# Gated mix of linear attention and feed-forward: the first loads cut into halves of rows over two queues

## The chip, the cores and the metric

The kernel runs on one core of a Trainium2 chip. The metric is device time in microseconds (us) of one execution, the median of several runs; lower is better. Beside the times there is one profiled execution, with every instruction of every engine and the traffic of the DMA queues.

## The reference

For one sequence of 2048 tokens of width 640 the kernel mixes two branches with a gate per token:

```python
qkv = x @ wqkv                                   # 32 heads of 20
phi(t) = concat(softmax(t @ w_phi), softmax(-t @ w_phi))
kv, z = phi(k).T @ v, sum over tokens of phi(k)  # linear attention
a = (phi(q) @ kv / (phi(q) @ z + 1e-6)) @ wo
b = silu(x @ w1) @ w2                            # width 1728
g = sigmoid(sum(x * gate_w))
out = g * a + (1 - g) * b
```

All inputs and the output are float32.

## The kernel before

Every float32 operand of a large product is split into a rounded part ("hi") and the remainder ("lo"), and each product is made of three passes, hi by hi, hi by lo and lo by hi (`PASSES`, line 57). `split` (line 113) does this: ScalarE (ACT) copies the source into the rounded tile, then VectorE (DVE) or GpSimd (POOL) subtracts it from the source. TensorE (PE) multiplies, SyncE (SP) issues nearly all loads.

The kernel has three long stages: keys and values of 16 token tiles with their sums, then the feed-forward branch, then queries, attention and output. The change touches the very beginning of the first stage, lines 342 to 382, where the work is written out in order and `inorder` (line 122) holds PE, ACT, DVE and POOL to that order.

What stands there:

- Eight matmuls on a tile of ones (`warm`, line 284) run first; they need no input.
- `xT` is read in chunks of 128 of the 640 input features (c = 0 to 4), 256 tokens at a time. `x_loads` (line 162) is a generator: each `next(x0)` loads one chunk (`xra`, 128 KB) and splits it into `xa`, lo on POOL.
- `wv` holds the value weights and the gate column, 642 columns. Chunk 0 of it is the tile `wvr0`, called wv0 here (lines 343, 344, 347): the first 360 columns are loaded by the ACT queue, the other 282 by SP.
- The key weights are not read ready-made: `wkc` (320 KB a chunk) and `wkr` (the last heads, 48 rows) are multiplied on PE with a block-diagonal matrix of `w_phi` in `k_weights` (line 296, tile `pwk`), and the result is split into columns 0 to 639 of `wh` and `wl`. The block-diagonal matrix is expanded by one DVE instruction (line 355) from `bdc`.
- The order on PE is: values of chunk 0 for tokens 0 to 255 (`share(0, ...)`, twelve matmuls into `kvp` and `kvq`, in the three passes), key weights of chunk 0 (`pwk`, twelve matmul records), values of chunk 1, key weights of chunk 1, and so on. `v_weights` (line 328) loads the value weights of chunks 1 to 4 (`wvr1` to `wvr4`, 321 KB each) on SP.

Loads signal their landing on eight DMA semaphores in turn (DMAHW0 to DMAHW7), so a load's issuing instruction waits until the load eight places earlier in the program has landed.

Of the kernel before, what the change touches and what calls it, by code (L numbers as in the profile page):

```python
# [8 lines left out]
F32 = mybir.dt.float32  # L9
# [7 lines left out]
P = 128  # L17
S = 2048
D = 640
# [31 lines left out]
EB = 2  # L51
KXB = 1
WC = 2 * D + 2
CUTS = (0, 500, 1000, WC)
# [6 lines left out]
def mix_kernel(ctx: ExitStack, tc: tile.TileContext, xT, wqT, wkc, wkr, wv, bd, bdc, cst, wo, w1, w1r, w2, out):  # L61
    nc = tc.nc
# [6 lines left out]
    def opened(name, **kw):  # L69
        open_pools[name] = tc.tile_pool(name=name, bufs=1, **kw)  # L70
        return open_pools[name].__enter__()
# [7 lines left out]
    ta = opened("ta")  # L79
# [14 lines left out]
    def raw(name):  # L94
        return wp.tile([P, D + 2], F32, tag="raw", name=name, bufs=4)

    def slot(name, pool=None, tag="x", bufs=7):
        return (pool or wp).tile([P, 2, 512], F32R, tag=tag, name=name, bufs=bufs)
# [14 lines left out]
    def split(hi, lo, src, lo_eng="dve"):  # L113
        nc.scalar.copy(hi, src)  # L114
        eng = nc.vector if lo_eng == "dve" else nc.gpsimd
        eng.tensor_tensor(lo, src, hi.bitcast(F32), op=ALU.subtract)  # L116
# [4 lines left out]
    @contextmanager  # L121
    def inorder(*engines):

        traced = nc.cur_bb.bb.instructions
        n = len(traced)
        yield
        prev = {}
        for i in traced[n:]:
            if i.engine in engines:
                if i.engine in prev:  # L130
                    tc.add_manual_dep(
                        i,
                        prev[i.engine],
                        mybir.DependencyInfo(mybir.DependencyClass.NoSync, mybir.DependencyReason.DATA),
                        reason="inorder",
                    )
                prev[i.engine] = i.name
# [7 lines left out]
    warms = cp.tile([P, 1], F32, name="warms")  # L145
# [3 lines left out]
    st0 = [t[:, k * D : (k + 1) * D] for t in stf for k in range(3)][:NC]  # L149
# [3 lines left out]
    onesf = ta.tile([P, P], F32, name="onesf")  # L153
# [4 lines left out]
    g_d = dp.tile([NT, P], F32, name="g_d")  # L158

    X = {}  # L160

    def x_loads(phase, u, tiles=None):

        tiles = [] if tiles is None else tiles
        for c in range(0, NC, 1 if phase == "f" else 2):
            r = raw(f"xr{phase}_{u}_{c}")[:, :512]
            t = slot(f"x{phase}_{u}_{c}")
            if phase == "f":
                nc.sync.dma_start(r, xT[c * P : (c + 1) * P, u * 512 : (u + 1) * 512])
                split(t[:, 0, :], t[:, 1, :], r)  # L170
                tiles.append(t)
            else:
                n = min(2, NC - c)
                tiles += [t[:, :, k * 256 : (k + 1) * 256] for k in range(n)]
                step = n if u else 1
                for k in range(0, n, step):
                    cols = slice(k * 256, (k + step) * 256)
                    nc.sync.dma_start(
                        r[:, cols].rearrange("p (c s) -> p c s", s=256),
                        xT[(c + k) * P : (c + k + step) * P, u * 256 : (u + 1) * 256].rearrange("(c p) s -> p c s", p=P),  # L180
                    )
                    split(t[:, 0, cols], t[:, 1, cols], r[:, cols], "pool")
                    if k + step < n:
                        yield
            yield
        X["f" if phase == "f" else "t", u] = tiles

    def load_x(phase, u):
        for _ in x_loads(phase, u):
            pass  # L190

    def x_of(t):
        return [x[:, :, t % 2 * P : (t % 2 + 1) * P] for x in X["t", t // 2]]

# [14 lines left out]
    def xb_split(p):  # L209
# [4 lines left out]
        if c == 0:  # L214
            X["t", u] = []
        X["t", u].extend(t[:, :, k * 256 : (k + 1) * 256] for k in range(r.shape[1] // 256))

# [78 lines left out]
    def k_weights(c, half):  # L296

        g0, g1 = ((0, 4), (4, GR))[half]
        bank = ps.tile([P, 512], F32, tag=f"pwk{half}", name=f"pwk{c}_{half}", bufs=2 - half)
        for gi in range(g0, g1):  # L300
            n = min(GW, D - gi * GW)
            r = st0[c][:n, gi * P : (gi + 1) * P] if gi < NG else strest[:n, c * P : (c + 1) * P]
            lo = (gi - g0) * GW
            nc.tensor.matmul(bank[:, lo : lo + n], r, bdt[:n, gi, :n], start=True, stop=True)  # L304
        return bank

    def k_split_w(c, half, bank):
        lo, hi = ((0, 4 * GW), (4 * GW, D))[half]
        split(wh[:, c, lo:hi], wl[:, c, lo:hi], bank[:, : hi - lo])

    def kv_share(c, todo):

        for hx, hw in PASSES:
            for t, lo, hi, opens in todo:
                nc.tensor.matmul(  # L315
                    kv_cols(t, lo, hi),
                    x_of(t)[c][:, hx, :],
                    WKV[hw][:, c, lo:hi],
                    start=(opens and hx == 0 and hw == 0),
                    stop=(c == NC - 1 and hx == 1),  # L320
                    skip_group_check=True,
                )

    X["t", 0] = []
    x0 = x_loads("a", 0, X["t", 0])
    kvp1 = [None] + [ps.tile([P, 512], F32, name=f"kvq{k}") for k in (1, 2)]

    def v_weights(c):
        r = ta.tile([P, 2 * D], F32, tag="e", name="wvr1", bufs=EB)[:, : D + 2] if c == 1 else flat(f"wvr{c}") if c == 2 else raw(f"wvr{c}")
        nc.sync.dma_start(r, wv[c * P : (c + 1) * P, :])  # L330
        split(WKV[0][:, c, D:], WKV[1][:, c, D:], r)

    def values(t):
        return [(t, D, CUTS[2]), (t, CUTS[2], WC)]

    def keys(t):
        return [(t, 0, CUTS[1]), (t, CUTS[1], D)]

    def share(c, cols, opens=()):
        kv_share(c, [(*p, p in opens) for p in cols])  # L340

    with inorder(PE, ACT, DVE, POOL):
        wv0 = ta.tile([P, 2 * D], F32, tag="e", name="wvr0", bufs=EB)[:, : D + 2]
        nc.scalar.dma_start(wv0[:, : CUTS[2] - D], wv[:P, : CUTS[2] - D])
        nc.scalar.dma_start(st0[0], wkc[0])
        next(x0)
        nc.sync.dma_start(wv0[:, CUTS[2] - D :], wv[:P, CUTS[2] - D :])
        nc.sync.dma_start(bdct, bdc)
        nc.sync.dma_start(strest[: wkr.shape[0], :], wkr)
        for lo, hi in ((D, CUTS[2]), (CUTS[2], WC)):  # L350
            split(WKV[0][:, 0, lo:hi], WKV[1][:, 0, lo:hi], wv0[:, lo - D : hi - D])
        cols = [p for pair in zip(values(0), values(1)) for p in pair]
        share(0, cols, cols)
        blocks = bdt[:, :, :GW].rearrange("p g (j f) -> p g j f", f=DH)
        nc.vector.tensor_tensor(
            blocks,
            bdct[:GW, : GR * DH].rearrange("p (g f) -> p g f", f=DH)[:, :, None, :].to_broadcast([GW, GR, GR, DH]),
            bdct[:GW, GR * DH :][:, None, :, None].to_broadcast([GW, GR, GR, DH]),
            op=ALU.mult,
        )  # L360
        for c in range(NC):
            if c + 1 < NC:
                next(x0)
                v_weights(c + 1)
                nc.sync.dma_start(st0[c + 1], wkc[c + 1])
            for half in range(2):
                k_split_w(c, half, k_weights(c, half))
            if c == 0:
                share(1, values(0) + values(1))
            elif c < 3:  # L370
                share(c - 1, keys(0), keys(0)[:1] if c == 1 else ())
            else:
                share(c - 1, [(0, lo, hi) for lo, hi in zip(CUTS, CUTS[1:])])
        share(NC - 1, [(0, lo, hi) for lo, hi in zip(CUTS, CUTS[1:])])
        kvp1[0] = ps.tile([P, 512], F32, tag="pwk0", name="kvq0", bufs=2)
        for k, (lo, hi) in enumerate(zip(CUTS, CUTS[1:])):
            for c in range(NC):
                if c > 1 or k == 0:
                    kv_share(c, [(1, lo, hi, c == 0)])
                elif k == 1:  # L380
                    kv_share(c, [(1, lo, D, False)])
        load_x("a", 1)
# [180 lines left out]
    phs, eks = {}, {}  # L563
    X["f", 0] = []
    xf0 = x_loads("f", 0, X["f", 0])
    with inorder(ACT, DVE, POOL):
        for t in range(NT - 1):
# [123 lines left out]
    r = raw("w1rr")  # L691
# [4 lines left out]
    r = raw("w2rr")  # L696
# [637 lines left out]
```

## Time and profile before

| what | us |
|---|---|
| median of 3 runs (lowest, highest) | 764.87 (764.68, 765.44) |
| the profiled execution's own time | 765.65 |
| its span, first to last instruction | 763.9 |
| PE busy | 757.3 |
| first matmul on real data starts | 5.59 |
| second half of wv0 is cast | 6.15 |
| first key-weight matmul starts | 8.17 |

The span begins with the first instruction; times in the rows are microseconds from there. A line of the timeline gives start, duration, engine, line, operation, output and inputs with their shapes, and in brackets how long the engine had idled before and what released it. ACTq and SPq are the instructions with which those engines issue DMAs; they are not counted as busy.

### The profile page before, as it was taken

The page shows a single profiled execution, that of the slowest core. Times are in us where ns is not written, and L with a number is a line of the kernel's source. Part 1 is how long each engine was busy: PE and PEld are TensorE (multiplying, and loading weights), DVE is VectorE, ACT ScalarE, POOL GpSimd, SP SyncE. Part 2 cuts the span into 40 slices and gives each one's busy share as a digit, 9 for nine tenths or more (in the row PEclk, how much of TensorE's full clock was granted, in tenths as well). Part 3 has the DMA queues.
Part 4 walks back from the last instruction along what each step waited for, and adds up shares of the span by engine and source line. Part 5 has one row for each costly group of instructions (what it writes and reads, how often), then busy time and mean ns, then how long its engine had stood idle before and what let it go on. Part 6 is the DMA issues. An engine that isn't in the chain of part 4 may idle for free.

```text
span 763.9 us, 10660 instructions
## 1 busy us (share of the span) xinstructions
PE 757.3 (99%) x4259; PEld 666.6 (87%) x4259; DVE 370.3 (48%) x662; ACT 267.5 (35%) x484; POOL 263.0 (34%) x163
## 2 busy tenths in 40 slices
PE   8999999999999999999999999999999999999998
PEld 7888888888888888888888888888899999999998
DVE  5676666676641221112211122123587888787761
ACT  5444444336542211122211222133454443334341
POOL 2488777758000000000000000001166766855641
PEclk9999999999999999999999999999999999999999
DMA  7111111112650220002200025022004222111222
GB/s 254 52 53 53 52 52 53 60 46 85 206 174 1 70 82 1 1 0 72 84 0 1 1 68 160 17 65 86 15 1 158 91 75 71 53 52 43 70 70 91
DMA packets 35454, 50.36 MB, mean 66 GB/s; under 512 B 3539, under 2 KB 23267, under 8 KB 35405
## 3 DMA queue, kind: packets, MB, share of 16 engines
q1 hardware_dynamic: 35117, 49.18, 20.5%
q8 instruction: 33, 0.54, 0.3%
q10 hardware_dynamic: 288, 0.51, 0.3%
q14 instruction: 16, 0.13, 0.1%
HBM read 38.56 MB, written 11.11 MB: 65 GB/s over the span
## 4 chain that ended last, share of the span: by engine, by line
PE 92%; POOL 2%; DVE 2%; DMA 2%; issue 1%; ACT 1%; SPq 0%; POOLq 0%; DVEq 0%
PE acc L684 22%; PE ph L503 22%; PE kvp L456 16%; PE pa L1069 9%; PE pq L414 8%; PE pn L1026 3%; PE kv L426 2%; PE pT L951 2%; PE kvp L519 2%; PE kvp L315 1%; PE kvq L315 1%; PE pwk L304 1%; POOL eq L813 1%; POOL ez L777 1%; DMA wvr<-wv 1%
## 5 line engine op out<-in xcount | busy, mean ns | idle before, releaser
L116 POOL TENSOR_TENSOR xb<-xrb,xb 128x512 fp32r<-128x512 f32 (+1 forms) x18 | 19.9, 1130 | 342.1 <-ACT xb L114 338.4
L116 DVE TENSOR_TENSOR u<-ph,u 128x512 fp32r<-128x512 f32 x48 | 33.2, 691 | 178.0 <-ACT u L114 177.9
L684 PE MATMUL acc<-u,w 128*128 128x512 f32 x480 | 114.8, 392 | 0.1
L684 PEld LDWEIGHTS acc<-u,w 128*128 128x128 f32 x480 | 89.5, 188 | 19.3 <-ACT u L114 0.5
L503 PE MATMUL ph<-xf,w 128*128 128x512 f32 x420 | 99.8, 390 | 0.0
L505 ACT ACTIVATE ph<-ph 128x512 f32<-128x512 f32 x48 | 27.9, 582 | 189.2 <-PE ph L503 189.2
L503 PEld LDWEIGHTS ph<-xf,w 128*128 128x128 f32 x420 | 78.7, 188 | 16.7
L456 PE MATMUL kvp<-wh,xa 128*128 128x500 f32 (+1 forms) x420 | 93.0, 357 | 0.0
L456 PEld LDWEIGHTS kvp<-wh,xa 128*128 128x128 f32 x420 | 71.6, 188 | 9.8
L1069 PE MATMUL pa<-oT,wo 120*128 120x256 f32 x600 | 76.8, 282 | 0.0
L1069 PEld LDWEIGHTS pa<-oT,wo 120*128 120x128 f32 x600 | 73.7, 188 | 0.0
L684 PE MATMUL acc<-u,f 128*128 128x512 f32 x300 | 73.3, 394 | 0.0
L503 PE MATMUL ph<-xf,f 128*128 128x512 f32 x300 | 72.7, 394 | 0.0
L503 PEld LDWEIGHTS ph<-xf,f 128*128 128x128 f32 x300 | 56.4, 188 | 13.1
L684 PEld LDWEIGHTS acc<-u,f 128*128 128x128 f32 x300 | 56.2, 188 | 13.0
L777 POOL TENSOR_TENSOR ez<-eq,zbc 128x1280 f32<-128x1280 f32 x16 | 48.0, 3000 | 38.3 <-ACT eq L763 38.0
L116 POOL TENSOR_TENSOR ph<-ek,ph 128x1280 fp32r<-128x1280 f32 x16 | 47.5, 2966 | 27.9 <-ACT ph L114 27.9
L414 PE MATMUL pq<-wq,xb 128*128 128x320 f32 x360 | 55.4, 311 | 0.0
L414 PEld LDWEIGHTS pq<-wq,xb 128*128 128x128 f32 x360 | 53.0, 188 | 0.0
L456 PE MATMUL kvp<-wl,xa 128*128 128x500 f32 (+1 forms) x210 | 47.4, 356 | 0.0
L813 POOL TENSOR_TENSOR eq<-eq,sm 128x1280 f32<-128x1280 f32 x16 | 37.9, 2367 | 21.1 <-DVE sm L807 17.6
L484 POOL TENSOR_TENSOR ek<-ek,st 128x1280 f32<-128x1280 f32 x16 | 37.9, 2369 | 9.2 <-issue 6.1
(159 smaller groups left out, 1105.2 us busy)
## 6 DMA issues: line engine op xcount, KB each, us to landing
wr<-w SPq DMA_DIRECT2D x26, 320.0 KB, 3.1
xrf<-xT SPq DMA_DIRECT2D x20, 256.0 KB, 3.6
fb_d<-o SPq DMA_DIRECT2D x20, 256.0 KB, 2.3
y<-fb_d SPq DMA_DIRECT2D x16, 256.0 KB, 3.2
out<-y SPq DMA_DIRECT2D x16, 256.0 KB, 2.3
xra<-xT SPq DMA_DIRECT2D x14, 256.0 KB, 2.6
xrb<-xT SPq DMA_DIRECT2D x12, 256.0 KB, 2.7
xra<-xT SPq DMA_DIRECT2D x12, 128.0 KB, 2.9
```

What stands on the lines that cost most here:

```text
L116: eng.tensor_tensor(lo, src, hi.bitcast(F32), op=ALU.subtract)
L315: nc.tensor.matmul(kv_cols(t, lo, hi), x_of(t)[c][:, hx, :], WKV[hw][:, c, lo:hi], start=(opens and hx == 0 and hw == 0), stop=(c == NC - ...
L414: nc.tensor.matmul(dst, xt[c][:, hx, :], w[:, c, hw, lo : lo + n], start=first, stop=(hx == 1 and c == NC - 1))
L456: nc.tensor.matmul(kv_cols(t, lo, hi), xt[c][:, hx, :], WKV[hw][:, c, lo:hi], start=(n == 0), stop=(n == 3 * NC - 1), skip_group_check=True,)
L484: nc.gpsimd.tensor_tensor(groups(e), groups(e), spread(st[:, 1, :]), op=ALU.mult)
L503: nc.tensor.matmul(ph, lhs, rhs, start=(n == 0), stop=(n == len(todo) - 1))
L505: nc.scalar.activation(hs, ph, AF.Silu)
L684: nc.tensor.matmul(acc[m], lhs, rhs, start=(f == order[0] and n == 0), stop=(f == order[-1] and n == len(todo) - 1))
L777: nc.gpsimd.tensor_tensor(ez, Q[t]["e"], zbc, op=ALU.mult)
L813: nc.gpsimd.tensor_tensor(groups(q["e"]), groups(q["e"]), spread(q["sm"][:, 2 * H : 4 * H]), op=ALU.mult)
L1026: nc.tensor.matmul(pns[u, gp][:GW, a, :], kvw_of(hk, 2 * i + jj)[:w], f[:w, hp, jj * 256 : (jj + 1) * 256], start=(n == 0), stop=(n == 3 * ...
L1069: nc.tensor.matmul(pa[:, a, :], WO[:GW, c, hw, ds] if c < NG else WOR[:, ds], o[:, ho, c, :], start=(k == 0), stop=(k == len(todo) - 1),)
```

## The change

The tile of wv0 is made earlier. A helper `both` issues a load as two, rows 0 to 63 on SP and rows 64 to 127 on ACT. The first chunk of `xT` and the whole of wv0 are loaded that way, wv0 behind the chunk on both queues. `wkc` of chunk 0 moves from the ACT queue to SP, behind `bdc` and ahead of `wkr`. ACT gets a one-column copy into `warms` ahead of its first cast. The split of wv0 keeps its two column parts.

```diff
     X = {}
+    wv0 = ta.tile([P, 2 * D], F32, tag="e", name="wvr0", bufs=EB)[:, : D + 2]
+
+    def both(dst, src):
+
+        for eng, rows in ((nc.sync, slice(0, P // 2)), (nc.scalar, slice(P // 2, P))):
+            eng.dma_start(dst[rows], src[rows])
 
     def x_loads(phase, u, tiles=None):
...
                 for k in range(0, n, step):
                     cols = slice(k * 256, (k + step) * 256)
-                    nc.sync.dma_start(
-                        r[:, cols].rearrange("p (c s) -> p c s", s=256),
-                        xT[(c + k) * P : (c + k + step) * P, u * 256 : (u + 1) * 256].rearrange("(c p) s -> p c s", p=P),
-                    )
+                    if u == 0 and c + k == 0:
+                        both(r[:, cols], xT[:P, :256])
+                    else:
+                        nc.sync.dma_start(
+                            r[:, cols].rearrange("p (c s) -> p c s", s=256),
+                            xT[(c + k) * P : (c + k + step) * P, u * 256 : (u + 1) * 256].rearrange(
+                                "(c p) s -> p c s", p=P
+                            ),
+                        )
+                    if u == 0 and c + k == 0:
+                        both(wv0, wv[:P, :])
+                        nc.scalar.copy(warms, onesf[:, :1])
                     split(t[:, 0, cols], t[:, 1, cols], r[:, cols], "pool")
...
     with inorder(PE, ACT, DVE, POOL):
-        wv0 = ta.tile([P, 2 * D], F32, tag="e", name="wvr0", bufs=EB)[:, : D + 2]
-        nc.scalar.dma_start(wv0[:, : CUTS[2] - D], wv[:P, : CUTS[2] - D])
-        nc.scalar.dma_start(st0[0], wkc[0])
         next(x0)
-        nc.sync.dma_start(wv0[:, CUTS[2] - D :], wv[:P, CUTS[2] - D :])
         nc.sync.dma_start(bdct, bdc)
+        nc.sync.dma_start(st0[0], wkc[0])
         nc.sync.dma_start(strest[: wkr.shape[0], :], wkr)
```

SP's queue at the beginning, before. `xra` is the input chunk, `wvr` value weights, `stage` the space for key weights, `bdc` and `wkr`:

```order
L178 DMA xra_0_125<-xT 128x256
L347 DMA wvr_122<-wv 128x282
L348 DMA stage_93<-bdc 128x126
L349 DMA stage_92<-wkr 48x640
L178 DMA xra_0_125<-xT 128x256
L330 DMA wvr_153<-wv 128x642
L365 DMA stage_92<-wkc 128x640 [waits DMAHW0_49]
L178 DMA xra_2_182<-xT 128x256 [waits DMAHW1_49]
```

The same place with the change:

```order
L166 DMA xra_0_123<-xT 64x256
L166 DMA wvr_100<-wv 64x642
L358 DMA stage_93<-bdc 128x126
L359 DMA stage_92<-wkc 128x640
L360 DMA stage_92<-wkr 48x640
L187 DMA xra_0_123<-xT 128x256
L344 DMA wvr_155<-wv 128x642 [waits DMAHW0_49]
L376 DMA stage_92<-wkc 128x640 [waits DMAHW1_49]
L187 DMA xra_2_184<-xT 128x256 [waits DMAHW2_49]
```

`wkc` of chunk 0 stands ahead of the second input chunk, there is one load more in all, and so the load of `wvr1` (L344) now waits for DMAHW0, the first half of the first input chunk; before, it waited for nothing.

ACT at the beginning, its two loads and its first casts, before (`wh<-wvr_122` is wv0, `wh<-wvr_153` is `wvr1`):

```order
L344 DMA wvr_122<-wv 128x360
L345 DMA stage_92<-wkc 128x640
L114 ACT_TABLE_LOAD
L114 CAST xa_0_126<-xra_0_125 128x256 [waits DMAHW1_49]
L114 CAST wh<-wvr_122 128x360 [waits DMAHW0_49]
L114 CAST wh<-wvr_122 128x282 [waits DMAHW2_49]
L114 CAST xa_0_126<-xra_0_125 128x256 [waits DMAHW6_49]
L114 CAST wh<-wvr_153 128x642 [waits DMAHW7_49]
```

With the change:

```order
L166 DMA xra_0_123<-xT 64x256
L166 DMA wvr_100<-wv 64x642
L195 ACT_TABLE_LOAD
L195 COPY warms<-onesf 128x1 [waits DVE_49]
L114 CAST xa_0_124<-xra_0_123 128x256 [waits DMAHW1_49,DMAHW0_49]
L114 CAST wh<-wvr_100 128x360 [waits DMAHW3_49,DMAHW2_49]
L114 CAST wh<-wvr_100 128x282
L114 CAST xa_0_124<-xra_0_123 128x256 [waits DMAHW7_49]
L114 CAST wh<-wvr_155 128x642 [waits DMAHW0_49]
```

The table load stands where it stood, third on the engine. The first cast of wv0 waits for both halves of its rows, all columns; the second waits for nothing more. On PE, DVE and POOL the order of the computing instructions is that of before, from first to last. On SP, near the end of the program, one load of a partial sum from `fb_d` stands ahead of one output store that it used to follow.

## Rows read from the trace of the kernel before

**Rows 1.** The page, part 1: busy time, share of the span, instructions.

```profile
PE 757.3 (99%) x4259; PEld 666.6 (87%) x4259; DVE 370.3 (48%) x662; ACT 267.5 (35%) x484; POOL 263.0 (34%) x163
```

**Rows 2.** Chain of waits from 0 to 60: start us, us, what.

```profile
1.19 4.93 DMA wvr<-wv
...
6.63 0.39 PE kvp L315
```

**Rows 3.** Waits of PE, whole run: total us, times, longest us.

```profile
PE kvp L315 <- ACT wh L114: 1.2, 2, 0.8
...
PE pn L1026 <- DVE fT L969: 0.4, 1, 0.4
```

**Rows 4.** Timeline from 0 to 11: start us, us, what, [idle before, releaser].

```profile
1.05 3.78 PE L284 MATMUL warm<-ones 128*128 128x512 f32 x8 [1.05 <-DVE ones L154]
...
1.64 1.28 ACT L114 ACT_TABLE_LOAD   x1 [1.64 <-PEq L1325]
...
3.10 0.43 SPq L330 DMA_DIRECT2D wvr<-wv  x1
4.57 0.33 SPq L365 DMA_DIRECT2D stage<-wkc  x1
4.75 0.40 ACT L114 CAST xa<-xra 128x256 fp32r<-128x256 f32 x1 [1.82 <-DMA xra<-xT]
...
5.06 0.49 ACT L114 CAST wh<-wvr 128x360 fp32r<-128x360 f32 x1
5.23 0.73 POOL L116 TENSOR_TENSOR xa<-xra,xa 128x256 fp32r<-128x256 f32 x1 [3.93 <-ACT xa L114]
5.58 0.78 DVE L116 TENSOR_TENSOR wl<-wvr,wh 128x360 fp32r<-128x360 f32 x1 [3.67 <-ACT wh L114]
...
5.59 0.43 PE L315 MATMUL kvp<-wh,xa 128*128 128x360 f32 x1 [0.76 <-ACT wh L114]
...
6.15 0.43 ACT L114 CAST wh<-wvr 128x282 fp32r<-128x282 f32 x1 [0.61 <-DMA wvr<-wv]
...
6.61 0.45 DVE L116 TENSOR_TENSOR wl<-wvr,wh 128x282 fp32r<-128x282 f32 x1 [0.26 <-ACT wh L114]
...
6.98 0.90 DVE L355 TENSOR_TENSOR stage<-stage 120x720 f32<-120x720 f32 x1
...
7.91 0.73 ACT L114 CAST wh<-wvr 128x642 fp32r<-128x642 f32 x1 [0.41 <-DMA wvr<-wv]
...
8.17 1.61 PE L304 MATMUL pwk<-stage,stage 120*128 120x120 f32 x12
...
8.67 0.83 DVE L116 TENSOR_TENSOR wl<-wvr,wh 128x642 fp32r<-128x642 f32 x1 [0.79 <-ACT wh L114]
...
10.29 0.32 PEld L315 LDWEIGHTS kvp<-wl,xa 128*128 128x128 f32 x2
```

**Rows 5.** DMA from 0 to 40: GB/s in slices of 1 us; issues, KB each, us to landing.

```profile
GB/s 0 29 126 291 388 320 317 386 363 299 327 351 396 400 190 55 276 192 136 149 200 0 0 0 0 211 146 259 39 0 0 0 0 0 0 0 0 0 0 8
...
wvr<-wv SPq DMA_DIRECT2D x4, 321.0 KB, 4.8
...
xra<-xT SPq DMA_DIRECT2D x7, 128.0 KB, 4.6
stage<-wkc ACTq DMA_DIRECT2D x1, 320.0 KB
...
wvr<-wv ACTq DMA_DIRECT2D x1, 180.0 KB
wvr<-wv SPq DMA_DIRECT2D x1, 141.0 KB
stage<-wkr SPq DMA_DIRECT2D x1, 120.0 KB
stage<-bdc SPq DMA_DIRECT2D x1, 63.0 KB, 4.6
```

**Rows 6.** DMA from 216.4 to 220.4: GB/s in slices of 0.1 us; a load of 64 rows.

```profile
GB/s 13 0 0 0 0 0 0 0 0 0 0 0 0 0 51 77 154 77 154 307 410 410 231 179 102 282 358 353 333 333 389 184 266 287 287 287 185 62 61 61
...
w2rr<-w SPq DMA_DIRECT2D x2, 160.0 KB, 3.0
```

## The prediction, made before the run

> **What bounds the kernel.** I read the busy shares first. PE is busy 757.3 of 763.9 us [rows 1], so only some 6.6 us of the span can be had by making it wait less. Then the waits of PE: the largest is 1.2 us in two pieces, for casts of `wh` at the very beginning, and the next behind it are 0.4 us and less, far down the program and not touched [rows 3]. Then the chain of waits: it starts with the load of wv0's second part, issued at 1.19 and landed 4.93 us later, at about 6.13, and from 6.63 on it runs through PE [rows 2]. So until 6.63 the kernel is bound by a landing; after it, by PE. What an earlier landing gives is kept to the end if no later load is then late, because PE's order is unchanged and hardly anything else stops it.
>
> The timeline shows the place. The warm-up matmuls end at 4.83. The first input chunk lands at about 4.72 (its cast starts at 4.75), wv0's first 360 columns are cast at 5.06, and PE starts its first pair at 5.59. Then it waits: the other 282 columns are cast only at 6.15. The `lo` subtractions and the expansion of the block matrix follow on DVE until 6.98 + 0.90 = 7.88, and the first key-weight matmul starts at 8.17 [rows 4]. I call the landing of all of wv0 V, and the start of that key-weight matmul K. K was 8.17; V was 6.13.
>
> **Term 1, when wv0 lands.** Before, the loads in flight beside the chunk (128 KB) and wv0 (180 + 141 KB) included 320 KB of `wkc` on ACT's queue [rows 5]. That now stands behind them on SP. So 449 KB, 460 thousand bytes, come first. The rate of the opening slices (29, 126, 291, 388 GB/s, 1 us each) has moved 446 thousand bytes by 4.0 and 460 by 4.04 [rows 5]. Landing comes later than this mean: the chunk and wv0's first part are 308 KB, 315 thousand bytes, which the same row has moved by 3.55, and they landed at 4.57 (the issue that waited for wv0's part) and 4.72 [rows 4], 1.0 and 1.2 us later. That gives V = 5.0 to 5.2; I take 5.1. Bounds: not before 4.6, where 308 KB had landed, and not after 6.13.
>
> **Term 2, from V to the key weights.** Two chains run side by side. DVE: the 360-column cast starts at V + 0.03 and takes 0.49; the subtraction of 360 columns took 0.78 while POOL worked from 5.23 to 5.96 [rows 4]. Now the chunk lands earlier and POOL's subtraction is over by then, so I take 0.53, interpolated between 0.45 for 282 columns and 0.83 for 642 [rows 4]; 0.78 is the other end. With 0.03 for each hand-over and 0.08 of overlap between neighbours on DVE, as at 6.98, the 282 columns end at V + 1.50, the expansion (0.90) at V + 2.32, and PE can start at V + 2.4. PE: first pair at V + 0.55, the second at V + 0.90 (its cast is now queued right behind the first), the wl pairs as DVE delivers them at V + 1.14 and V + 1.54, and the pass over `xa`'s lo part ends at about V + 2.4 too. So K = V + 2.4 = 7.5, and the gain is 8.17 - 7.5 = 0.67. With 0.78 for the subtraction it is 0.42.
>
> **Term 3, what must be there by then.** By the same row and 1.1 us of lag: `bdc` (512 KB in all) lands at 5.3, wanted by DVE at 6.5; `wkc` (832 KB) at 6.2, wanted at 7.5; `wkr` (952 KB) at 6.5, wanted after 8. They cost nothing, with 1 us in hand. The tight one is `wvr1`. The bytes ahead of it are the same as before, 1401 KB with its own; the row has moved these 1435 thousand bytes by 6.9, and its cast started at 7.91 [rows 4]. Its subtraction ended at 8.67 + 0.83 = 9.50, and PE loaded the weights that need it at 10.29 [rows 4]: 0.8 us in hand. So the gain is capped at 0.8, and 0.67 passes under it. If the slice after 4.0 loses the second queue and falls from 388 to the 320 behind it, `wvr1` lands 0.2 later and the cap is 0.6.
>
> **Terms at nothing.** The copy into `warms` stands in ACT's idle stretch of 1.82 us ahead of its first cast; a 256-column cast is 0.40, so this is less [rows 4]. The table load ran at 1.64, before any data came, and does so again: "ahead" brings nothing. Two more issues on SP (0.4 us each as the neighbours [rows 4]) delay nothing that is not queued behind bytes anyway. The load that changed places near the end has no row that waits for it. The new wait of `wvr1`'s issue for the first half chunk holds it from 3.10 to about 4.2, and the loads behind it on SP; the queue still has `bdc` to the second chunk to move, 631 KB, so it does not run dry.
>
> Sum: 0.67 us. The profiled execution took 765.65, 0.78 above the median; with the change it would be 764.98, and the median 764.87 - 0.67 = 764.2.
>
> **Rivals.**
> *The second block binds (slower).* `wvr1` was issued at 3.10 and landed 4.8 us later [rows 4, 5]. If it keeps 4.8 from an issue at 4.2, it lands at 9.0; cast, hand-overs and subtraction (1.62) end at 10.6, against 10.29 before: 0.3 slower, 765.2. It decides from a landing at 8.7 on. Against it: most of the 4.8 was queueing behind earlier bytes. Chance 0.08.
>
> *A half of the rows moves at half the rate (slower).* If each half ran at 194 GB/s and one behind the other, 460 thousand bytes would take 2.4 us in place of 1.2, V would be 6.3 and K 8.7: 0.5 slower, 765.4; it decides from V = 5.8. The row that speaks against it: two loads of 64 rows, 160 KB each. The slices from the first 51 to the second 410 add up to 164 thousand bytes, the first load alone, and its last two slices ran at 410 [rows 6]. Chance 0.05.
> The Trainium skill, page SBUF — State Buffer, section Door 1: The DMA port swizzle, says that a DMA's bandwidth depends on how many of the 16 ports its partitions reach; rows 0 to 63 reach eight. By that rule a half alone would go at half rate; the 410 GB/s disagree.
>
> *One queue is slower than two.* From 4.0 on all traffic is SP's. If every slice then ran at the lowest one, 299 [rows 5], `wvr1`'s bytes would be through at 7.3 and landed at 8.3: the cap falls to 0.4, time 764.5. For it: the slices drop from 388 to 320 just after ACT's queue had its last load. Against: 386 and 363 with SP alone. Chance 0.15.
>
> *The lag shrinks.* With nothing beside the first loads V = 4.6 and `wvr1` lands 0.4 earlier: gain 1.2, time 763.7. Chance 0.15.
>
> **How the numbers follow.** The forecast, 764.2 with 763.9 to 764.6 of its own, has 0.57. The range for 8 in 10 takes in the forecast, the single-queue case, most of the shrunken lag and part of the second block, with the 0.4 us by which runs of one kernel differ: 763.5 to 765.2. A measurement of this kernel can tell about 0.2%, 1.5 us. Only a gain over all the cases here would be faster by that (0.05); slower needs more than either slow case gives (0.03); the same has 0.92.
>
> **What would show it.** Right: wv0's casts back to back from about 5.1, no PE wait between the first and second pair longer than 0.2, first key-weight matmul near 7.5, `wvr1` cast near 7.9 and no wait on it above 0.2. The chain of waits would still begin with wv0, about 1 us shorter. Wrong: a cast of wv0 after 5.8, or PE waiting for `wl` of chunk 1, or a key-weight matmul that waits for `wkc`.

## The result and the profile after

The change took 766.51 us (median of 19 runs, 765.60 to 767.25), the kernel before on the same chip 764.92 (19 runs, 764.57 to 767.23): ratio 1.0018, 95% interval [1.0012, 1.0024], 1.6 us slower. The forecast was 764.2 with 763.5 to 765.2. The profiled execution took 766.39 with a span of 764.6; before 765.65 and 763.9.

PE's busy time is that of [rows 1], so the difference is waiting:

```profile
PE 757.2 (99%) x4259; PEld 666.7 (87%) x4259; DVE 370.1 (48%) x662; ACT 267.6 (35%) x485; POOL 262.9 (34%) x163
```

The timeline of the change, 0 to 14, columns as in [rows 4]:

```profile
0.73 0.57 ACTq L166 DMA_DIRECT2D xra<-xT  x1
...
0.74 0.57 SPq L166 DMA_DIRECT2D xra<-xT  x1
...
1.33 0.61 ACTq L166 DMA_DIRECT2D wvr<-wv  x1
1.36 0.84 SPq L166 DMA_DIRECT2D wvr<-wv  x1
...
2.25 0.59 SPq L358 DMA_DIRECT2D stage<-bdc  x1
2.89 0.43 SPq L359 DMA_DIRECT2D stage<-wkc  x1
...
3.36 0.59 SPq L360 DMA_DIRECT2D stage<-wkr  x1
3.98 0.40 ACT L114 CAST xa<-xra 128x256 fp32r<-128x256 f32 x1 [0.53 <-DMA xra<-xT]
3.99 0.42 SPq L187 DMA_DIRECT2D xra<-xT  x1
4.46 0.43 SPq L344 DMA_DIRECT2D wvr<-wv  x1
...
5.32 0.82 ACT L114 CAST wh<-wvr 128x360 fp32r<-128x360 f32 x2 [0.94 <-DMA wvr<-wv]
...
5.86 0.43 PE L329 MATMUL kvp<-wh,xa 128*128 128x360 f32 x1 [1.03 <-ACT wh L114]
...
7.17 0.33 PE L329 MATMUL kvp<-wh,xa 128*128 128x360 f32 x1
7.34 0.33 PE L329 MATMUL kvq<-wh,xa 128*128 128x360 f32 x1
...
7.76 1.61 PE L318 MATMUL pwk<-stage,stage 120*128 120x120 f32 x12
...
9.65 0.73 ACT L114 CAST wh<-wvr 128x642 fp32r<-128x642 f32 x1 [1.17 <-DMA wvr<-wv]
...
10.43 0.56 PE L329 MATMUL kvp<-wh,xa 128*128 128x360 f32 x2 [1.06 <-ACT wh L114]
...
11.30 0.30 PEld L329 LDWEIGHTS kvp<-wl,xa 128*128 128x128 f32 x2 [0.27 <-DVE wl L116]
```

The first part went as forecast. The chunk is cast 0.77 earlier than in [rows 4] (4.75), wv0's two casts stand back to back at 5.32, and the first key-weight matmul starts at 7.76 where it was 8.17: 0.41 gained. Then the gain is lost. SP's issues took 0.57, 0.84, 0.59 and 0.59 where the whole load in [rows 4] took 0.43, one issue more (`wkc`) stands ahead, and `wvr1` is issued at 4.46, not 3.10. It is cast at 9.65, not 7.91, and PE idles 1.06 before the second block of values. A second, smaller wait follows in the last line: the subtraction of the late `wvr1` holds the weight load for `wl` by 0.27.

The chain of waits of the change (start, us, what) names the same load:

```profile
3.99 0.42 SPq L187
...
4.46 5.17 DMA wvr<-wv
```

It no longer begins with wv0, as in [rows 2], but runs along SP's issues from 0.74 and then waits 5.17 for `wvr1`. The waits of PE grew by that piece, 2.1 in two pieces against 1.2 in [rows 3]:

```profile
PE kvp L329 <- ACT wh L114: 2.1, 2, 1.1
```

DMA of the change, 0 to 40, GB/s in slices of 1 us, and then the slice from 4 to 5 alone, queue by queue (packets, MB, share of 16 engines):

```profile
GB/s 0 0 123 303 137 270 285 234 318 282 355 401 403 400 402 234 83 295 182 122 139 220 0 0 0 0 200 153 258 45 0 0 0 0 0 0 0 0 0 0
```

```profile
DMA packets 182, 0.14 MB, mean 137 GB/s; under 512 B 153, under 2 KB 153, under 8 KB 182
...
q1 hardware_dynamic: 182, 0.14, 80.5%
```

The same slice of the kernel before:

```profile
DMA packets 300, 0.39 MB, mean 388 GB/s; under 512 B 103, under 2 KB 208, under 8 KB 300
...
q1 hardware_dynamic: 204, 0.18, 53.3%
q10 hardware_dynamic: 96, 0.21, 52.2%
```

Before, `wkc` ran on ACT's queue (q10) beside SP's small packets. Now SP's queue (q1) is alone, and 153 of its 182 packets are under 512 B, the 504-byte rows of `bdc` and the 4-byte signals: the data of `wkc`, issued until 3.32, is hardly there yet. By the sizes in the trace, 14 of the other 29 packets are wv0's last rows and 15 the first of `wkc`. The 80.5% says that the engines were not empty: those 15 packets took 0.32 us each in the mean, where the first 15 of `wkc` before took 0.10. Why they were slow no run here shows. By 8.0 the row adds up to 1352 thousand bytes, before to 1857 [rows 5]. The 1435 thousand that end with `wvr1` had moved by 6.9 before and by 8.3 now, and each time its cast followed 1.0 and 1.4 later.

Behind these two waits nearly all of the delay stays: 0.99 at 11.70 (10.71 before), 0.80 at 523.58, 0.73 at the last matmul (761.03 against 760.31). In the traces of this study the execution's own time is 5.32 to 5.51 more than the start of the last matmul, so a difference of the first 13 us is the difference of the run to about 0.3 us.

### The profile page after: what moved, and what is told of

Its sections match the earlier page's. It is cut to its first block, busy times and chain, and to the rows that moved or that the text cites. A ratio compares the mean times of both kernels' runs of the same rounds, so it can differ in the third digit from the quotient of the medians.

```text
span 764.6 us, 10661 instructions
## 1 busy us (share of the span) xinstructions
PE 757.2 (99%) x4259; PEld 666.7 (87%) x4259; DVE 370.1 (48%) x662; ACT 267.6 (35%) x485; POOL 262.9 (34%) x163
## 4 chain that ended last, share of the span: by engine, by line
PE 89%; DVE 4%; POOL 3%; issue 1%; DMA 1%; ACT 0%; SPq 0%; POOLq 0%; DVEq 0%; ACTq 0%
PE acc L695 23%; PE ph L514 23%; PE kvp L467 16%; PE pa L1080 7%; PE pq L425 7%; PE pn L1037 3%; PE kv L437 2%; PE kvp L530 2%; PE pT L962 2%; PE kvp L329 1%; POOL eq L824 1%; POOL ez L788 1%; DVE sm L791 1%; PE kvq L329 1%; PE pwk L318 1%
```

## The experiments

Two theories went into the expectations. **Queue** (W, in the first ones T, where an expectation uses a letter; its rival Q there blames the move of `wkc` alone): the halves make SP's issues dear, with `wkc` in the queue as well all that follows is late, and PE waits for `wvr1`. **Clock** (C): the longer idle stretch of PE before its first pair (1.03 against 0.76 in [rows 4]) lets TensorE's clock rise later. The rows show the level: 360-column matmuls start 0.30 apart at the lower level (360 / 0.30 us = 1.2 GHz) and 0.17 apart, as at 7.17 and 7.34 above, near the upper (2.4 GHz). The granted clock of the profile reads 1.00 in both kinds of stretch (7.3 to 9.0 and 11.5 to 13.0 of the change's second trace), so the level is read from the spacing alone. "Ten warm-ups" means `WARM = 10` for 8, which shortens that idle stretch or fills it. Ratios are against the kernel before on the same chip, its median between 764.68 and 764.80.

### Whole loads again, the key weights left on SP

```diff
-                        both(r[:, cols], xT[:P, :256])
+                        nc.sync.dma_start(r[:, cols], xT[:P, :256])
...
-                        both(wv0, wv[:P, :])
+                        nc.scalar.dma_start(wv0, wv[:P, :])
```

> The change with its halves undone: the first input chunk whole on SP, the whole first value weights on ACT, the key weights of chunk 0 still on SP. Theory T: SP's issues take 0.40 to 0.45 each again, the second value weights are issued near 3.1 and land between 7.9 and 8.3; time within 0.4 us of the kernel before or up to 0.8 faster. Rival Q: landing after 9.0 as with the change, time 1.0 to 1.6 above the kernel before.

Measured 764.93 (11 runs), ratio 1.0005 [0.9996, 1.0014]. Timeline of that run:

```profile
3.08 0.92 SPq L344 DMA_DIRECT2D wvr<-wv  x1
...
7.62 0.73 ACT L114 CAST wh<-wvr 128x642 fp32r<-128x642 f32 x1 [0.40 <-DMA wvr<-wv]
...
9.31 0.56 PE L329 MATMUL kvp<-wh,xa 128*128 128x360 f32 x2
```

Its DMA row, GB/s in slices of 1 us from 0:

```profile
GB/s 0 39 185 278 405 291 299 298 369 401 392 399 399 349 86 162 297 78 181 274 8 0 0 0 27 236 204 189 1 0 0 0 0 0 0 0 0 0 0 0
```

Without the halves `wvr1` is issued at 3.08 and cast at 7.62, PE does not wait for it, and the loss is gone. `wkc` is on SP here too, and the slice from 4 to 5 moved 405 where the change moved 137: `wkc` on SP, the one queue it leaves and the small rows of `bdc` are therefore not enough to cause the loss.

### One part of the change at a time

Key weights moved to SP, the rest as before:

> The kernel before with one part of the change alone: the key weights of chunk 0 move from ACT's queue to SP, behind the block weights; the value weights stay in two column parts. Theory T: one more issue of 0.43, the second value weights issued near 3.55, landed near 8.3, inside the 0.8 us that they had in hand; time within 0.4 us of the kernel before. Rival Q: landing after 9.0 and 1.0 to 1.6 slower.

Measured 765.38 (11), ratio 1.0010 [1.0001, 1.0019]: `wvr1` is issued at 3.54 and cast at 8.33, early enough. The 0.7 us above before (764.68) is more than the 0.4 that was expected; its trace shows no wait of PE for it, and the cause stays open. Halves kept, `wkc` back on ACT:

```diff
+                        nc.scalar.dma_start(st0[0], wkc[0])
...
-        nc.sync.dma_start(st0[0], wkc[0])
```

> The change with one part undone: the key weights of chunk 0 go back to ACT's queue, behind ACT's two halves. Theory T (SP's issues are late: a half-row load takes 0.57 to 0.84 us to issue instead of 0.40 to 0.44, and one issue was added): the load of the second value weights is issued about 0.5 us sooner than with the change, near 4.0, and lands near 9.0; the time stays 0.3 to 1.0 us above the kernel before. Rival Q (the 320 KB of key weights left ACT's queue, so one queue carries everything): landing back at 7.9, time 0.3 to 0.8 us under the kernel before.

Measured 766.91 (6), ratio 1.0025 [1.0013, 1.0037]. `wvr1` is cast at 8.21 and PE does not wait for it, and yet this is the slowest so far. In its trace the 360-column matmuls stay 0.30 apart until the key weights, which start at 9.28 and take 1.96, not 1.61:

```profile
9.28 1.96 PE L319 MATMUL pwk<-stage,stage 120*128 120x120 f32 x12
```

What this trace shows is the late clock, and no wait for `wvr1`. Neither theory of the expectation had 2.2 us slower with the load in time. Only wv0 in halves, all else as before:

```diff
-        nc.scalar.dma_start(wv0[:, : CUTS[2] - D], wv[:P, : CUTS[2] - D])
+        nc.scalar.dma_start(wv0[P // 2 :], wv[P // 2 : P, :])
...
-        nc.sync.dma_start(wv0[:, CUTS[2] - D :], wv[:P, CUTS[2] - D :])
+        nc.sync.dma_start(wv0[: P // 2], wv[: P // 2, :])
```

> The kernel before with one part of the change alone: the first value weights in two halves of rows over SP and ACT instead of two column parts; the input chunk stays whole, the key weights stay on ACT. Theory W (a half-row load is dear to issue): SP's second issue and ACT's first take 0.55 to 0.85 us instead of 0.40 to 0.44, the second value weights are issued 0.3 to 0.8 later, near 3.6, and land near 8.4; time 0 to 0.6 us above the kernel before. Rival (issues are slow only with the whole change): issues of 0.45 or less, time within 0.2.

The times fell into two groups, five runs at 764.80 to 765.38 and five at 766.52 to 767.08 (one run of 1256.46 left out), ratio 1.0013 [1.0003, 1.0022]. Timeline of its profiled execution (765.09):

```profile
0.74 0.55 ACTq L344 DMA_DIRECT2D wvr<-wv  x1
0.74 0.40 SPq L178 DMA_DIRECT2D xra<-xT  x1
...
1.20 0.56 SPq L347 DMA_DIRECT2D wvr<-wv  x1
...
1.32 0.60 ACTq L345 DMA_DIRECT2D stage<-wkc  x1
...
1.80 0.57 SPq L348 DMA_DIRECT2D stage<-bdc  x1
...
5.82 0.43 PE L315 MATMUL kvp<-wh,xa 128*128 128x360 f32 x1 [0.99 <-ACT wh L114]
```

The 64-row halves took 0.55 and 0.56 to issue, the whole chunk 0.40, and the issue behind each half 0.57 and 0.60 as well. PE idled 0.99 before its first pair, nearly as in the change. This trace is of the faster group; the slower one, outside the expected 0 to 0.6 above before, has no trace.

### The clock: the idle stretch filled

The change, the kernel before, and the two halved versions just shown, each with ten warm-ups:

> The kernel before with only the first value weights loaded half by half of their rows, and ten warm-up matmuls in place of eight. Theory that the two groups of times of this edit (764.8 to 765.4 and 766.5 to 767.1) are TensorE's clock, which falls behind the idle stretch of 0.99 us before the first pair: with ten warm-up matmuls that stretch is 0.2 to 0.5 us, the 360-column matmuls stand 0.17 us apart by 8 us, and all runs lie in 764.7 to 765.5, median 765.0. Rival, that the groups have another cause (a load that lands late in some runs): both groups stay, median 765.5 to 766.6.

Measured 765.12 (11 runs, 764.94 to 765.61), ratio 1.0002 [0.9994, 1.0011]. The slower group is gone, as the clock theory expected. In its trace PE still idles 0.66 before the first pair, and the clock is at the upper level from that pair on.

> The change with ten warm-up matmuls. Theory W plus C (the late second value weights cost about 1 us in every run, a late clock adds to it in some): the wait of PE before the second block stays at 0.8 to 1.2 us, the time falls only to 765.4 to 766.2 and scatters less. Clock alone: 764.5 to 765.2. Late load alone: 766.3 to 766.7, as the change.

Measured 766.05 (11 runs, 765.49 to 766.63), ratio 1.0011 [1.0002, 1.0019]. PE idles 0.21 before the first pair and `wvr1` is still late:

```profile
8.33 1.61 PE L318 MATMUL pwk<-stage,stage 120*128 120x120 f32 x12
...
9.22 0.73 ACT L114 CAST wh<-wvr 128x642 fp32r<-128x642 f32 x1 [0.78 <-DMA wvr<-wv]
...
10.00 0.56 PE L329 MATMUL kvp<-wh,xa 128*128 128x360 f32 x2
```

The time is the expected one, the wait is not: the 0.78 is idle time of ACT. PE was expected to wait 0.8 to 1.2 before the second block and waits less than 0.1 there (the key weights end at 9.94), since TensorE's clock rose only at about 7 in this trace, so that PE comes to that block later itself; `wl` then holds a weight load by 0.27.

> The kernel before with ten warm-up matmuls. Theory C: its idle stretch of 0.76 us made the clock late in few runs only, so little changes: within 0.4 us of the kernel before, or up to 0.4 faster. If its clock were often late as well: 0.5 to 1.5 faster. If the added matmuls delay real work: up to 0.4 slower.

Measured 764.86 (12), ratio 0.9996 [0.9987, 1.0004]: the median of the kernel before gains nothing from it.

> The kernel with halves and the key weights back on ACT's queue, with ten warm-up matmuls instead of eight, so that PE idles some 0.2 us instead of 1.07 before its first real matmul. Theory C (in that kernel it was not a load but TensorE's clock, which rose only at about 10.0, after that idle stretch): the clock is at its upper level before the key weights begin, and the time falls by 1.2 to 2.0 us to 764.5 to 765.5. Rival H (loads in halves are themselves slower, the clock is beside the point): the time stays within 0.4 of 766.9.

Measured 765.94 (12), ratio 1.0016 [1.0007, 1.0025], 1.0 less than without the two warm-ups. That misses the expected fall of 1.2 to 2.0: 1.1 us above the kernel before are left. Its trace (767.59, of the two slowest runs) still has PE idle 0.96, since wv0 landed only at 6.1, and the late clock; of what holds the other runs there is no trace.

### The halves, with the clock's part taken out

The first experiment of this chapter once more, with ten warm-ups. Against the change with ten warm-ups it differs in the halves alone.

> The change with whole loads in place of the halves, key weights still on SP, and ten warm-up matmuls. Against the change with ten warm-up matmuls (766.05) this differs in the halves alone. Theory that the halves make the issues of the start dear and the queue late: wvr1 issued by 3.2 and landed by 7.7, no wait of PE for it over 0.1 us, median 764.4 to 765.1, some 1.0 us below 766.05. Rival, that the loss of the change is the clock alone and so already gone at ten warm-up matmuls: 765.8 to 766.2.

Measured 765.12 (11 runs, 764.58 to 765.73), ratio 1.0003 [0.9994, 1.0012]: 0.93 below 766.05, and `wvr1` is issued at 3.09 and cast at 7.86. The two stem from two chips, on which the kernel before took 764.80 and 764.79. Timeline:

```profile
8.06 1.61 PE L318 MATMUL pwk<-stage,stage 120*128 120x120 f32 x12
```

So of the 1.7 us from 764.8 to 766.5 the halves cost 0.9, and some 0.4 to 0.5 went with the two warm-ups (766.51 to 766.05, two chips). The last 0.3, from 764.8 to 765.12, no interval here tells from nothing. The two traces show where the halves cost: the first key weights start 0.27 later with them (8.33 against 8.06), behind a wv0 that is cast 0.37 later (5.36 against 4.99), and the second ones 0.67 later (12.15 against 11.48), behind a `wvr1` that is cast 1.36 later. Both landings have a part in it. The halves bring one issue more on SP and dearer issues at once, and no run parts these two.

### Is it the late issue of `wvr1` alone?

The kernel before with `wvr1`'s issue held until the first chunk has landed (one column copied into its tile first), and the change with ten warm-ups and `wvr1` issued early (`bdc` and `wkc` on ACT, `wkr` behind `wvr1`):

> The kernel before with the suspected cost added alone: the load of the second value weights cannot be issued before the first input chunk has landed (a one-column copy into its tile by DVE), so SP issues it near 4.95 instead of 3.10; no halves, nothing moved. Theory W: it lands between 8.8 and 9.8, PE waits for it, 0.5 to 1.3 us slower than the kernel before. Rival (the late issue is harmless, since bytes queue anyway): landing by 8.5, within 0.2 us.

Measured 765.00 (11), ratio 1.0003 [0.9994, 1.0011].

```profile
4.32 0.33 SPq L332 DMA_DIRECT2D wvr<-wv  x1
...
7.40 1.61 PE L306 MATMUL pwk<-stage,stage 120*128 120x120 f32 x12
...
8.20 0.73 ACT L114 CAST wh<-wvr 128x642 fp32r<-128x642 f32 x1 [0.78 <-DMA wvr<-wv]
```

Issued at 4.32, nearly as late as in the change, it is cast at 8.20, as the rival expected: a late issue alone is harmless when the loads ahead of it have already gone out, here by 3.01, in the change by 4.41.

> The change with its halves, but with SP's third and fourth place given to the second input chunk and the second value weights; ACT takes the block weights and the key weights of chunk 0, the last heads' rows come behind on SP; ten warm-up matmuls keep the clock out of it. Theory W: second value weights issued near 2.8, landed by 8.2, no PE wait for them; time 764.6 to 765.5. Rival H (halves are slow in themselves, wherever they stand): 765.9 or more, as the change with ten warm-up matmuls (766.05).

Measured 767.35 (8 runs, one of 4304.47 left out), ratio 1.0029 [1.0019, 1.0039], the slowest of all.

```profile
2.89 0.43 SPq L346 DMA_DIRECT2D wvr<-wv  x1
...
9.34 1.69 PE L320 MATMUL pwk<-stage,stage 120*128 120x120 f32 x12 [0.86 <-DMA stage<-wkc]
...
9.45 0.73 ACT L114 CAST wh<-wvr 128x642 fp32r<-128x642 f32 x1 [1.62 <-DMA wvr<-wv]
```

Issued at 2.89, `wvr1` is cast at 9.45 all the same, and PE waits 0.86 for `wkc`. The 764.6 to 765.5 of theory W is missed by far; the time is on the side of the rival, that the halves are slow wherever they stand. So the theory "issued late, therefore landed late" fails for this one load in both directions, and that the dear issues are what makes the stream late is argued from the rows, not shown. In this run twelve of `wvr1`'s 16 parts had signalled their landing by 7.76 and the last four came between 8.35 and 9.43; of `wkc`'s, 13 had by 7.45 and three came from 8.70 on. Why stays open.

### Other orders of whole loads

Both column parts of wv0 and `wkc` on ACT; and SP with the chunks and `wvr1` only, the rest on ACT:

> The kernel before with one load moved: the second column part of the first value weights goes from SP to ACT, ahead of the key weights of chunk 0; no load in halves of rows, SP has one issue less. Theory W (SP's issue time decides when the second value weights come): they are issued near 2.6 and land near 7.6, the first value weights are whole by 5.2, and the time is 0.2 to 0.8 us under the kernel before. If landings in unprofiled runs are already earlier than the profiles show, it is within 0.2 of it.

Measured 765.45 (11), ratio 1.0007 [0.9999, 1.0016], where 0.2 to 0.8 faster was expected; `wvr1` is cast at 7.51, but `bdc` was now issued behind the second chunk, and the key weights waited for its expansion until 7.70.

> Whole loads, and SP's queue kept for the data that PE needs next: the first input chunk, the second one and the second value weights in SP's first three places; ACT issues the whole first value weights, the block weights, the key weights of chunk 0 and the last heads' rows. Theory T: second value weights issued near 1.65 and landed before 7.5, so they no longer bind; the first value weights share the traffic with them and land between 5.3 and 6.0, first key-weight matmul 7.7 to 8.4, time between 0.5 faster and 0.3 slower than the kernel before. Rival Q gives no other number here.

Measured 765.46 (11), ratio 1.0014 [1.0005, 1.0022], where at most 0.3 slower was expected; `wvr1` is cast at 6.81, and the traced execution (767.29) had the late clock. No order beat the kernel before.

### More traces of both kernels

> The change once more, one look. Theory of the late queue: wvr1 issued at 4.3 to 4.6, its cast starts at 9.2 to 9.8, PE waits 0.7 to 1.2 us for it at the second block, whatever the clock does; traffic from 4 to 7 us 600 to 800 thousand kB/us slices together against 1025 before. If the clock also rises late (360-column matmuls 0.30 us apart until about 10 us), the span is above 765.5, otherwise 764.4 to 765. Rival, that the late landing of the first trace was chance: wvr1's cast before 8.5 and no wait of PE.

It took 767.22. Timeline:

```profile
5.59 0.82 ACT L114 CAST wh<-wvr 128x360 fp32r<-128x360 f32 x2 [1.05 <-DMA wvr<-wv]
...
8.44 0.51 PE L329 MATMUL kvp<-wh,xa 128*128 128x360 f32 x1
...
8.74 0.51 PE L329 MATMUL kvq<-wh,xa 128*128 128x360 f32 x1
...
9.13 0.73 ACT L114 CAST wh<-wvr 128x642 fp32r<-128x642 f32 x1 [0.59 <-DMA wvr<-wv]
...
9.51 2.10 PE L318 MATMUL pwk<-stage,stage 120*128 120x120 f32 x12
...
11.54 0.57 PE L329 MATMUL kvp<-wh,xa 128*128 128x360 f32 x2
```

`wvr1` is late again (9.13), but here PE is at 1.2 GHz until the key weights and reaches the second block at 11.54, when `wvr1` has long been there: the late clock and the late load cover each other. Part of the expectation failed, then: PE does not wait for `wvr1` "whatever the clock does".

The next two expectations were written for the kernel before, but the traces taken for them are of the change, so they were not tried:

> The kernel before, a third trace. In all traces so far the last matmul and the execution's own time stand 5.33 to 5.43 us apart, and whatever differs between two kernels arises before 13 us. So a usual run of before (764.8) must start some 0.8 us faster than the profiled one (765.65): both parts of wv0 landed by about 5.2 in place of 6.13, first key-weight matmul at about 7.4 in place of 8.17. Theory: a trace of before with a time of 764.4 to 765.1 shows just that, and then the room that the prediction counted (0.67 us) was there in the profiled execution alone. Rival: a trace with such a time still shows V near 6 and K near 8, and the 0.8 us lies elsewhere.

> The same once more, since a trace may fall on an execution of 765.5 or more again (as two of two did): then V is near 6 with K near 8, or the 360-column matmuls stand 0.30 us apart until 9 us or later, and the time follows the shift of the second block of value weights against 9.71 us to 0.2 us.

The traces serve as the change's third and fourth trace: 767.23 (clock late, `wvr1` cast at 10.07) and 766.10 (clock early, cast at 9.27, PE waits 0.48). In all four, wv0 is cast between 5.32 and 5.63, `wvr1` between 9.13 and 10.07, and the slice from 4 to 5 moves 122 to 157.

> The kernel before once more, for a second trace: the same landings within 0.3 us (first chunk near 4.7, all of the first value weights near 6.1, second value weights near 7.9), no wait of PE for the second block; the rise of the clock may stand elsewhere, since the records so far have it at 4.4 to 10.4 us.

> The kernel before, a third trace of it. Two traces of it so far took 765.65 and 766.67, both above its median of 764.8, and what differs between kernels arises before 13 us. Theory that the room counted in the prediction was in the profiled execution alone: a trace at 764.4 to 765.1 shows both parts of wv0 landed by about 5.2 (6.13 in the profiled one), first key-weight matmul at 7.3 to 7.5 (8.17), as the trace with wvr1 held did (764.95). Rival: it shows V near 6 and K near 8 with such a time, and the difference lies elsewhere. If the execution falls at 765.4 or above again, V is near 6 or the clock rises late, and the question stays with the trace of the held wvr1.

These two are of the kernel before and took 766.67 and 766.63, both with the late clock. Timeline of the second:

```profile
5.98 0.43 ACT L114 CAST wh<-wvr 128x282 fp32r<-128x282 f32 x1 [0.49 <-DMA wvr<-wv]
...
8.16 0.50 PE L315 MATMUL kvp<-wh,xa 128*128 128x360 f32 x1
...
8.46 0.50 PE L315 MATMUL kvq<-wh,xa 128*128 128x360 f32 x1
...
9.23 1.81 PE L304 MATMUL pwk<-stage,stage 120*128 120x120 f32 x12
```

So the late clock is not the change's alone: it costs before 1.0 as well (766.6 against the profiled 765.65), and in its five sets of runs few are that slow (8 of 128 above 766.4). Two single runs of before beside these traces took 767.33 and 767.02, though; why runs taken singly came out slow is not shown. The question of the last expectation stays unanswered: all three traces of before are of executions 0.78 us or more above its median, so no trace shows a usual one.

## Why the prediction was wrong

The forecast was 2.3 us too low. By medians, 0.67 of it is a gain that did not come, 0.9 the cost of the halves, 0.4 to 0.5 what two more warm-ups take away, and 0.3 is not told from nothing.

- **Term 1, V = 5.1, within 5.0 to 5.2.** 5.30 in the change's trace, 5.5 to 5.6 in its three others, above the range in all. Mis-sized by 0.2 and more; the first issues took 0.57, not 0.40, so the first bytes moved after 2.0 (slices 0 and 123, before 29 and 126).
- **Term 2, K = V + 2.4.** 7.76 from 5.30 is V + 2.46: right. The gain at this point was 0.41, the forecast's lower case.
- **Term 3 failed, and it decided.** "The row has moved these 1435 thousand bytes by 6.9": it was 8.3. The way from bytes to landing held (1.4 behind in place of 1.1), but the row was taken over from a stream that was issued earlier and over two queues (with whole loads and `wkc` on SP it was 6.8). The cap that should have stood at 0.8 in hand became a wait of 1.06.
- **The step under it, "Two more issues on SP (0.4 us each as the neighbours [rows 4]) delay nothing that is not queued behind bytes anyway".** The count was wrong: up to `wvr1` it is one more, `wkc`. The price was wrong: 0.57 and 0.84 for the two halves, 0.59 for the issues of `bdc` and `wkr`. A row for it stood in the trace of before, beside the loads of 64 rows in [rows 6], which I had read for their rate alone. The view of that tile gives the issue in ns (least, median, most), against 0.33 and 0.43 us for 128 rows in [rows 4]:

```profile
L699 SPq DMA_DIRECT2D w2rr<-w x2: 558/571/584, 216.5 to 217.1; - x2
```

  And "delay nothing" did not hold: "so it does not run dry" counted bytes issued, not bytes that had begun to move: `wkc`, issued until 3.32, hardly moved before 5.
- **The new wait for the first half chunk** held nothing: that chunk's half had landed at 3.3, and the issue followed straight on the one ahead of it.
- **The rival "the second block binds"** was the mechanism, with its chance at 0.08. It put the issue at 4.2 and the landing at 9.0 (4.46 and 9.65 in the trace), but for the wrong reason, the semaphore; so its price, 0.3, was too small. From an issue at 4.46 its own sum gives a landing at 9.3 and 0.6 slower, still under the 1.6 measured.
- **The rivals on the rate** fell in their own form: the halves side by side moved 303 in the slice from 3 to 4 (before 291), so the pair did not go at half rate; one half by itself was not run. "One queue is slower than two" was nearer: the slice from 4 to 5 fell from 388 to 137, far below the 299 that was its bound; but one queue with whole loads moved 405 there.
- **The base, "the median 764.87 - 0.67".** The 0.67 was read from an execution 0.78 above the median. Since the rest of the run keeps what the start gives, a usual run of before must start some 0.8 earlier than the profiled one, and then had little of this gain left to give. Two runs agree: whole loads, in their trace 0.4 ahead of the traced before, are no faster in the median (1.0005), and the trace with `wvr1` held, at 764.95 itself a usual time, starts the key weights at 7.40, not 8.17. A trace of a usual run of before is lacking, so this stays an inference.
- **The clock** was in none of the cases. The two traces of the change with the late clock (767.22, 767.23) stand at the upper end of its times, which reach 767.25.

The Trainium skill, page Perfetto Trace Analysis, section What "DMA-bound" means, lists as one kind the issuing engine's track filled with DMA slices, a window that is descriptor generation and no data movement. The trace has such a track: SP issues from 0.74 to 4.89 with gaps of 0.04 to 0.06 only while the slices fall to 137. That the issuing is what bound is not shown: with the halves, `wvr1` issued at 2.89 was cast at 9.45 all the same.

## What to carry to other kernels

A load cut in two over two queues costs one of them a whole issue more, and here each half (64 rows) took longer to issue than the whole; price the issues one by one from rows of the same shape, and follow the last load that the queue must deliver in time, not the first. Bytes count from when they move, not from their issue: `wkc`'s issue ended at 3.32 in the change, its first packet started at 4.49, and the slice from 4 to 5 moved 137 with three more loads issued behind it by 4.89. And before a gain is taken off the median, see whether the profiled execution stands at the median: what it shows as idle may be its own excess. Last, idle time of the engine that casts is not idle time of the one that multiplies: read the wait where the loss would be.

## What the runs showed of the hardware that was not expected

- Issuing 64 rows took 0.54 to 0.84 us where 128 rows mostly took 0.39 to 0.48, on SP and ACT alike, and a whole load issued right behind a half took 0.57 to 0.61 too. Not every dear issue has a half before it: `wkr`, behind `wkc`, took 0.55 to 0.65 in the four traces of the change (0.43 before), and `wvr1` 0.92 in the run with whole loads.
- With the same first loads the clock rose at the first value matmuls in some executions and only about 10 us in others. In the 13 traces where PE idled 0.58 to 1.34 before the first pair, six have the early rise and seven the late one, and not by the length: 1.24 went early (the change, 766.10), 0.62 late (before, 766.67). In the seven where it idled 0.25 at most, the close spacing is there by 7.3. Against the profiled executions with the early clock it cost 1.0 us in the kernel before (766.6 against 765.65) and 0.8 in the change (767.2 against 766.4), where the late load hides a part. With two more warm-up matmuls no slow run was left for wv0 in halves. What decides it from run to run these runs don't show.
